# Moving a unit's part through the states next to the next unit's state sums

## Chip, cores, metric

One core of a Trainium2 chip. The metric is the device time of one execution in microseconds (us). Every run in this document was in the fast state, and every kernel timed or profiled gave correct results.

## The reference

```python
def _attn_ref(q, k, v, f_logit):                 # batch 4, heads 8, sequence 768, head_dim 48
    f = 1.0 / (1.0 + np.exp(-f_logit))
    for t in range(S):
        state = f[:, :, t, :, None] * state + np.einsum('bhd,bhe->bhde', k[:, :, t], v[:, :, t])
        y[:, :, t] = np.einsum('bhd,bhde->bhe', q[:, :, t], state)
def _moe_ref(x, w_a, w_b, w_out):                # 3072 x 384, d_ff 1536
    return ((x @ w_a) * (x @ w_b)) @ w_out       # x is y with its heads side by side
```

A gated linear attention feeds a bilinear feed-forward block. Everything is fp32.

## The kernel before

The attention is cut into 16 units of four heads and 384 positions. Head_dim is 48, so the attention's products use a quarter of the TensorE array, as 64-row tiles. The feed-forward's products use all of it (128x128 weights, 192 columns). They are the bulk of the work and are interleaved with the attention as "filler". The first units are written out by hand; from unit 4 on, a unit's work comes from this generator, whose pieces the scheduler takes up when its step counter passes the numbers given:

```python
    def slot(u):
        nxt = front(u + 1) if u + 1 < NU else iter(())
        next(nxt, None)
        yield
        if u > 2 * NQ:
            within(u - 1)        # L401: scores times v, 64-row, into ps_y
        if u < NU:
            scores(u)            # L319: k times q, 64-row, into ps_x; DVE masks
        next(nxt, None)
        yield
        if u < NU:
            turn(u)              # L347: six full 128x128 transposes; ACT copies kT (L351)
        if u > 2 * NQ:
            across(u - 1)        # L422: states times q, 64-row, adds into ps_y
        yield
        if u < NU:
            gains(u)             # L367: state sums, kT times v, 64-row; DVE adds
        yield
        # ... two more pieces of front(u + 1)

    def across(u):
        # ... L422 products into ps_y
        # ACT copies y out of ps_y in three copies (L435)
        # SyncE stores y into xT, the feed-forward's input (L450)
        # ... then load_unit(u + NSET): the loads of a later unit (L154, L156)
```

The filler is `up_pair` (L542, with ACT copies L550 to L559 and DVE adds L547) and `down` (L610). `down` writes its results into one tile `o` and stores that in two halves from SyncE (L645, L649). `begun_early` holds the step numbers of the first slots:

```python
        begun_early = (
            (22.9, 22.9, 24.5, 25, 26.3, 26.3),
            (27.3, 27.3, 27.8, 28.3, 29.8, 29.8),
            (30.3, 30.3, 31.3, 31.3, 32.3, 33.3),
            (33.4, 33.4, 33.9, 33.9, 36.1, 38.1),
            (39.1, 40.1, 41.1, 41.1, 42.1, 44.1),
        )
```

## Time and profile before

| | before |
|---|---|
| median of 3 runs | 630.34 us (629.26 to 631.24) |
| span of the profiled run | 628.2 us |
| PE busy | 592.5 us (94%) |
| DVE / ACT busy | 60% / 35% |

The prediction below shows and reads the lines that matter. Some things help in following it. PE is TensorE, ACT is ScalarE, DVE is VectorE, and SPq is the queue of SyncE, which issues transfers (DMA) here; tiles named ps_ are those that PE writes. A product of the program appears as two PE records (24 products of L422 as 48), a transpose as one. And the length of a PE record is modelled, so durations are read as differences of starts.

### The profile page before, as it was taken

What the parts mean: (1) busy time and instruction counts of PE and PEld (TensorE: products, weight loads), DVE (VectorE), ACT (ScalarE), POOL (GpSimd) and SP (SyncE); (2) the same over time, 40 slices, a digit from 0 to 9 for tenths busy, and PEclk for the clock granted to TensorE, in tenths of its full rate; (3) what the DMA queues carried; (4) which work ended last, traced back from release to release, by engine and by line L of the source; (5) the groups of instructions that cost most, each with busy time, mean ns of one, the idle gap of its engine ahead of it and who ended that gap; (6) DMA issues with size and microseconds to landing.
All of it is one profiled execution on the core that took longest, in us unless ns stands there. A gap on an engine that the chain in (4) does not pass through costs nothing.

```text
span 628.2 us, 13968 instructions
## 1 busy us (share of the span) xinstructions
PE 592.5 (94%) x5922; PEld 535.6 (85%) x5922; DVE 378.2 (60%) x748; ACT 221.3 (35%) x400; POOL 63.0 (10%) x58
## 2 busy tenths in 40 slices
PE   0859899999999999999999999999999999999995
PEld 0626555558998999999999999999999999999995
DVE  6868444797887567646675567647564344534541
ACT  6576498822332243224312242323311232022200
POOL 6243154410000000000000000000000000000000
PEclk9959999999999999999999999999999999999999
DMA  8786785000144404130404012040001000000000
GB/s 237 230 255 175 168 263 197 1 1 1 41 109 114 100 3 94 33 91 1 96 1 120 27 36 62 12 110 2 20 1 46 26 20 2 2 27 0 1 26 30
DMA packets 30343, 43.65 MB, mean 69 GB/s; under 512 B 3776, under 2 KB 24896, under 8 KB 30272
## 3 DMA queue, kind: packets, MB, share of 16 engines
q1 hardware_dynamic: 29984, 42.38, 25.0%
q8 instruction: 48, 0.79, 0.5%
q10 hardware_dynamic: 288, 0.30, 0.2%
q14 instruction: 23, 0.19, 0.1%
HBM read 33.23 MB, written 4.72 MB: 60 GB/s over the span
## 4 chain that ended last, share of the span: by engine, by line
PE 88%; DMA 4%; DVE 2%; ACT 2%; SPq 2%; issue 1%; ACTq 0%; DVEq 0%
PE ps_f L542 41%; PE ps_f L610 23%; PE ps_f L469 14%; DMA xT<-y 2%; PE ps_y L401 2%; PE ps_y L422 2%; PE ps_x L319 2%; PE ps_x L367 2%; PE ps_x L347 1%; SPq L154 1%; DMA raw<-in_moe_w_b_dram 1%; SPq L450 1%; DMA out_dram<-o 1%; ACT y L435 1%; DVE h L605 0%
## 5 line engine op out<-in xcount | busy, mean ns | idle before, releaser
L542 PE MATMUL ps_f<-xT,w_ba 128*128 128x192 f32 x864 | 155.4, 327 | 0.0
L547 DVE TENSOR_TENSOR groups<-ps_f,groups 128x384 f32<-128x384 f32 x144 | 80.1, 557 | 118.5 <-ACT groups L559 99.3
L542 PEld LDWEIGHTS ps_f<-xT,w_ba 128*128 128x128 f32 x864 | 142.3, 190 | 0.5
L469 PE MATMUL ps_f<-xT,w_ba 128*128 128x384 f32 x288 | 98.4, 502 | 7.9 <-DVE w_ba L216 5.9
L469 PEld LDWEIGHTS ps_f<-xT,w_ba 128*128 128x128 f32 x288 | 55.3, 195 | 47.8 <-DVE w_ba L216 7.0
L542 PE MATMUL ps_f<-b_sb,raw 128*128 128x192 f32 x432 | 82.0, 326 | 0.0
L542 PEld LDWEIGHTS ps_f<-b_sb,raw 128*128 128x128 f32 x432 | 72.2, 190 | 0.0
L550 ACT COPY groups<-ps_f 128x384 f32<-128x384 f32 x36 | 17.2, 478 | 109.3 <-PE ps_f L542 103.5
L610 PE MATMUL ps_f<-w_out,h 128*128 128x192 f32 x288 | 52.0, 330 | 0.3 <-DVE o L605 0.3
L610 PE MATMUL ps_f<-w_out,groups 128*128 128x192 f32 x288 | 50.9, 327 | 0.0
L610 PE MATMUL ps_f<-spare,h 128*128 128x192 f32 x288 | 49.6, 328 | 0.2 <-DVE h L605 0.2
L610 PEld LDWEIGHTS ps_f<-w_out,h 128*128 128x128 f32 x288 | 46.8, 190 | 1.3 <-DVE o L605 0.6
L610 PEld LDWEIGHTS ps_f<-w_out,groups 128*128 128x128 f32 x288 | 47.3, 190 | 0.1
L610 PEld LDWEIGHTS ps_f<-spare,h 128*128 128x128 f32 x288 | 46.7, 190 | 0.8 <-issue 0.5
L205 POOL TENSOR_SCALAR h<-h 128x768 f32<-128x768 f32 (+1 forms) x20 | 40.7, 2037 | 50.8 <-ACT h L202 50.8
L266 POOL TENSOR_SCALAR inv<-inv 128x768 f32<-128x768 f32 x14 | 13.5, 962 | 305.7 <-ACT inv L262 305.7
L605 DVE TENSOR_TENSOR o<-ps_f,u 128x192 f32<-128x192 f32 x36 | 12.8, 356 | 43.7 <-PE ps_f L610 40.8
L572 DVE TENSOR_TENSOR groups<-groups 128x384 f32<-128x384 f32 x72 | 36.6, 550 | 0.0
L559 ACT COPY groups<-ps_f 128x384 f32<-128x384 f32 x36 | 17.2, 478 | 52.7 <-PE ps_f L542 52.7
L542 PE MATMUL ps_f<-xT,raw 128*128 128x192 f32 x144 | 29.8, 330 | 0.0
L542 PE MATMUL ps_f<-b_sb,w_ba 128*128 128x192 f32 x144 | 29.3, 326 | 0.0
L319 PE MATMUL ps_x<-q_in,k_in 48*64 48x64 f32 x672 | 13.7, 226 | 16.2 <-DMA raw<-in_moe_w_b_dram 15.4
(113 smaller groups left out, 697.4 us busy)
## 6 DMA issues: line engine op xcount, KB each, us to landing
q_in<-in_q_dram SPq DMA_DIRECT2D x32, 144.0 KB, 4.0
k_in<-in_k_dram SPq DMA_DIRECT2D x32, 144.0 KB, 3.5
v_in<-in_v_dram SPq DMA_DIRECT2D x16, 288.0 KB, 5.1
raw<-in_moe_w_out_dram SPq DMA_DIRECT2D x6, 768.0 KB, 4.3
out_dram<-o SPq DMA_DIRECT2D x24, 192.0 KB, 1.9
f_in<-in_f_logit_dram SPq DMA_DIRECT2D x28, 144.0 KB, 3.0
xT<-y SPq DMA_DIRECT2D x46, 72.0 KB, 2.2
raw<-in_moe_w_b_dram SPq DMA_DIRECT2D x4, 768.0 KB, 7.2
```

What stands on the lines that cost most here:

```text
L205: nc.gpsimd.tensor_scalar(h, h, HI_MAX, None, ALU.min)
L266: nc.gpsimd.tensor_scalar(inv, inv, EXP_K, 1.0, ALU.mult, ALU.add)
L319: nc.tensor.matmul(ps[h][SUB * p:SUB * p + SUB, o:o + SUB], lhsT=kf[r, tokens(n, c, p)], rhs=qf[r, tokens(n, c, p)], start=True, stop=True,)
L367: nc.tensor.matmul(ps_x[R * h:R * h + D, p, (n * NC + c) * D:(n * NC + c) * D + D], lhsT=kT[r, n, c, R * h:R * h + D], rhs=t["v"][r, n, c, ...
L469: nc.tensor.matmul(ps[nm][:, 0:BLK], lhsT=w[:, kt, ft * 128:ft * 128 + 128], rhs=x[:, kt], start=kt == 0, stop=kt == NKT - 1,)
L542: nc.tensor.matmul(to[:, g], lhsT=w[:, g, j], rhs=x, start=start and g == 0, stop=True, skip_group_check=True)
L547: nc.vector.tensor_tensor(c[:, :, k, i], x, y, ALU.add)
L550: nc.scalar.copy(p1, x0)
L559: nc.scalar.copy(u3, x0)
L572: nc.vector.tensor_tensor(to[:, :, 2 * j + k], a[:, :, k], b[:, :, k], ALU.mult)
L605: nc.vector.tensor_tensor(to, x, y, op)
L610: nc.tensor.matmul(to, lhsT=x[:, i], rhs=w[:, i], start=first and i == 0, stop=i == HFT - 1, skip_group_check=True)
```

## The change

The states' part (`across`) moves from behind the transposes to just ahead of the next unit's state sums (`gains`). Both are 64-row products, so PE should enter and leave 64-row products twice a unit instead of three times.

```diff
         if u < NU:
             turn(u)
+        yield
         if u > 2 * NQ:
             across(u - 1)
-        yield
         if u < NU:
             gains(u)
```

## The prediction

> **What bounds the kernel now.** I read the page's busy shares first, then the table by stretches of time, then the list of instructions in order of time around the moved part, and last the SyncE queue. The first question is whether PE time is wall time where the change acts. In the table by stretches (columns: busy us and count of PE, PE's weight loads, DVE, ACT, POOL; granted clock; DMA share; GB/s):
>
> ```profile
> 60.00:147.00 87.00, 84.89 (x458) 50.47 (x460) 52.09 (x80) 57.87 (x84) 29.31 (x15) 1.00 0.41 116
> 147.00:205.00 58.00, 57.11 (x918) 54.39 (x908) 45.83 (x100) 16.13 (x32) 2.50 (x3) 1.00 0.29 73
> 205.00:540.00 335.00, 334.65 (x3453) 327.15 (x3452) 199.04 (x409) 94.83 (x195) 5.82 (x7) 1.00 0.17 42
> ```
>
> From 205 to 540 us PE is busy 334.65 of 335 us at full granted clock, DVE for 59% and ACT for 28%. PE is the bound there, and close to it from 147 to 205. The moved part runs only in those two stretches: the units before it, in the start-up, are written out by hand and are untouched. But "busy" says nothing of how densely PE issues, so I worked with starts. One unit of the attention (a unit is four heads of half a sequence), in PE's list in order of time (start, length, line, what, count; the length includes a modelled tail, so I use differences of starts):
>
> ```profile
> 325.98 0.89 PE L401 MATMUL ps_y<-at,v_in 64*48 64x64 f32 x48
> 326.69 0.92 PE L319 MATMUL ps_x<-q_in,k_in 48*64 48x64 f32 x48
> 327.54 2.22 PE L610 MATMUL ps_f<-w_out,h 128*128 128x192 f32 x12
> 329.59 0.82 PE L347 MATMUL ps_x<-ident,k_in 128*128 128x128 f32 x6
> 330.34 0.89 PE L422 MATMUL ps_y<-q_in,st 48*48 48x64 f32 x48
> 331.16 2.22 PE L610 MATMUL ps_f<-spare,groups 128*128 128x192 f32 x12
> 333.21 2.11 PE L610 MATMUL ps_f<-w_out,groups 128*128 128x192 f32 x12
> 335.26 0.74 PE L367 MATMUL ps_x<-v_in,kT 64*48 64x48 f32 x40
> ```
>
> L401 is the part within a block, L319 the scores, L347 the six transposes, L422 the part through the states (what moves), L367 the next unit's state sums. L610 and L542 are the big products of the other half of the kernel, interleaved as filler. The trace shows each fp32 product of the program as two records; I count records. A filler record costs 162.5 ns when undisturbed: in the same list elsewhere eight L542 records run from 203.87 to 205.17. So 12 should take 1.95 us, and what a stretch takes beyond that is the price of changing between full products and 64-row ones. Three changes into 64 rows are visible: at L401, L422, L367.
>
> **What the Trainium skill says.** "TensorEngine Tiling (Array Packing)", Key Properties: "Changing tiling mode (not just tile) drains the TensorE"; staying in a mode costs nothing of the kind. It gives no figure. The trace agrees and has the figures, about 0.1 us each, below. "TensorE: Matmul & The Clock Gate", Part 3, says products on different tiles of the array overlap and start some 4 ns apart; here 48 records of L422 start within 0.67 us, 14 ns apart on average, which agrees in kind. "Perfetto Trace Analysis", section Tensor Engine Instruction, says PE's end times are estimates, hence my use of starts, and that ACT and DVE are strictly in order, which matters for the rivals.
>
> **The change part by part.** No instruction is added or removed: 5,922 PE records stay. The comparison of the two programs' orders on PE shows nine places where L422 moves, always later, past 12 to 24 filler records. In eight of them it was directly after the transposes and now stands directly before L367. The ninth is the last unit, with no transposes before it and no sums after it. Three further units (those of about 185, 200 and 232 us) already had transposes, L422 and L367 in a row, so they don't change. The intent "two instead of three" thus holds for eight units, not twelve.
>
> What one of the eight saves, from starts:
> - Transposes followed by L422 took 330.34 - 329.59 = 0.75 us. Where a unit had no L422 (149.59, below) transposes followed by filler took 150.24 - 149.59 = 0.65. Saved: 0.093 (with the starts at ns).
> - L422 followed by filler took 331.16 - 330.34 = 0.82. A 64-row group followed by another 64-row group is L401 before L319: 326.69 - 325.98 = 0.71, and the same L401 followed by filler, in the last unit (506.59 to 507.40 below), takes 0.82. Saved: 0.110. L401 and L422 use the same order of tiles, so I take this over to L422 before L367.
> - Filler after L422 has one slow step besides: 24 records from 331.16 to 335.26 take 4.10 = 3.90 + 0.20, while in 149 to 153 us, with transposes before, 12 records take 2.04 = 1.95 + 0.094. The 0.094 is the entry into L367, which stays (as the entry into L422). Saved: 0.104.
>
> ```profile
> 149.59 0.82 PE L347 MATMUL ps_x<-ident,k_in 128*128 128x128 f32 x6
> 150.24 2.12 PE L610 MATMUL ps_f<-w_out,h 128*128 128x192 f32 x12
> 152.28 0.76 PE L367 MATMUL ps_x<-v_in,kT 64*48 64x48 f32 x48
> ...
> 506.59 0.89 PE L401 MATMUL ps_y<-at,v_in 64*48 64x64 f32 x48
> 507.40 1.57 PE L542 MATMUL ps_f<-xT,w_ba 128*128 128x192 f32 x8
> ```
>
> Sum 0.307 us a unit; all of it on PE, the bound. Eight units: **2.46 us**.
>
> There is one side gain. SyncE's queue is in order, and in the unit of 330 us it now holds an output store back behind the moved part's stores and the next loads:
>
> ```profile
> 332.31 3.79 SPq L450 DMA_DIRECT2D xT<-y  x5
> ...
> 339.16 0.42 SPq L156 DMA_DIRECT2D v_in<-in_v_dram  x1
> 339.68 0.42 SPq L649 DMA_DIRECT2D out_dram<-o  x1
> ...
> 343.86 0.36 DVE L605 TENSOR_TENSOR o<-ps_f,u 128x192 f32<-128x192 f32 x1 [2.84 <-DMA out_dram<-o]
> 344.27 1.89 PE L610 MATMUL ps_f<-w_out,h 128*128 128x192 f32 x10 [0.28 <-DVE o L605]
> ```
>
> DVE waits to write the single output tile o until that store has landed, and PE waits for DVE: 12 filler records from 341.88 to 344.27 take 2.39 instead of 1.95. In the changed program's SyncE order this L649 stands before the L450 stores. Its data is ready at 333.84 (end of the DVE step), so it should land near 336, eight us before it is needed. Gain **0.44 us**, once.
>
> One small loss: ACT copies y out after L422 in three copies (1.46 us), and the first-half copy of the next pair of products (L550, 0.48 us) now comes behind them in the last unit, with only filler between. Copies end about 2.4 us after L422 starts (475.76 + 1.46 against 474.80 in the unit of 474), L550 at 2.9; PE needs it 12 records after filler resumes: 0.82 + 0.10 + 1.95 = 2.87. With a semaphore's delay, up to 0.1 us. In the units that move before a pair, L367 lies between (0.67 us), so slack is 0.5.
>
> Sum: 2.46 + 0.44 - 0.1 = 2.8 us of 630.34.
>
> **The rivals.**
> 1. L367 waits where it now stands. Against the 36 ns assumed between L422 and L367, the three units that have them in a row show some 0.29 us (L422's last start to L367's first). But there the transposes' copy kT ends just before: in the unit of 185 us ACT's L351 runs 185.29 to 186.08 and L367 starts at 186.14. In the changed order 12 to 24 filler records, 2 to 4 us, lie between the copy and its reader. If the 0.29 was the array's after all, the saving is 0.05 a unit, and the time is 629.5.
> 2. ACT or the transfers become the bound: y's copies now collide with copies that the next products need, and xT arrives 2 to 4 us later. Against: the slack above; xT of the unit at 297 us lands near 305 and is read at 348; the last unit's lands at 518.8 and is read at 546. The next loads of the unit at 167 us move 2 us: f would land near 178 and is read at 179.5, the tightest of all. If several slipped, half a us each, the time is 629 to 631.
> 3. PE isn't the bound and nothing moves. The first fence speaks against it.
> 4. All three removed terms are larger than the neighbours tell, or more waits resolve like the one at 344 us (PE has one more of 0.8 us at 195, where the scores wait for DVE; that chain starts from PE, so it shifts along): 626.
>
> **Range and chances.** 630.34 - 2.8 = **627.5 us**, 0.4% less. The three timed runs of before spread over 2 us, which is most of the uncertainty; the medians of two kernels may differ by 1 us from that alone. Rivals 1 and 2 pull up to 629.5. Range 626.0 to 629.3. Faster by over 2% would need 12.6 us, more than all changes of mode together: 0.01. Slower by over 2% would need a new wait of 15 us: 0.01.
>
> **What would show it right or wrong.** In PE's list of the changed kernel: transposes to filler 0.65 us; L422 to L367 0.71 instead of 0.82 to filler; filler after transposes without the extra 0.2; at about 341 us no wait of DVE on out_dram. Wrong if L422 to L367 takes 0.95 as in rival 1, if a filler stretch after L367 shows a step over 0.3 us released by ACT, or if scores or L526 wait on DMA.

## The result

The kernel after took 626.58 us (median of 4 runs, 625.93 to 627.19) against 630.59 for the kernel before, measured beside it (629.26 to 631.24, 4 runs). The ratio is 0.9939, with a 95% interval from 0.9919 to 0.9959: a gain of 0.6%, small but clear of the noise. Ratios here are the mean time of one kernel's fast runs over that of the other's in the same rounds, so not quite the ratio of the medians. Both kernels were run again, twice for after: ratios 0.9943 (0.993 to 0.9956) and 0.9939 (0.9926 to 0.9952). The predicted 627.5 lay 0.9 us above the measured median; the predicted gain of 2.8 us stands against 3.6 to 3.8 by these ratios.

The same unit as in the prediction's second fence, in PE's list in order of time of the kernel after (start, length, what, count):

```profile
325.40 2.22 PE L610 MATMUL ps_f<-w_out,h 128*128 128x192 f32 x12
327.46 0.82 PE L347 MATMUL ps_x<-ident,k_in 128*128 128x128 f32 x6
328.11 2.12 PE L610 MATMUL ps_f<-spare,groups 128*128 128x192 f32 x12
330.07 2.11 PE L610 MATMUL ps_f<-w_out,groups 128*128 128x192 f32 x12
332.11 0.89 PE L422 MATMUL ps_y<-q_in,st 48*48 48x64 f32 x48
332.82 0.71 PE L367 MATMUL ps_x<-v_in,kT 64*48 64x48 f32 x40
```

The transposes now hand over to filler after 327.46 to 328.11 = 0.65 us (0.75 to L422 before). The 24 filler records take 332.11 - 328.11 = 4.00 (4.10). L422 hands over to L367 after 0.71 (0.82 to filler). L367 itself took 335.26 to 335.93 = 0.67 before and takes 332.82 to 333.46 = 0.64 now. The first three are the prediction's three terms; the fourth it didn't have. In five of the eight units the starts of L422 and L367 mix (last section), so the 0.71 can be read in three only; from transposes to the filler after L367 all eight gain 0.33 to 0.34 us.

SyncE in the same stretch of the kernel after, to be read against the prediction's fourth fence:

```profile
330.72 0.35 SPq L649 DMA_DIRECT2D out_dram<-o  x1
334.08 3.05 SPq L450 DMA_DIRECT2D xT<-y  x5
337.17 1.06 SPq L154 DMA_DIRECT2D f_in<-in_f_logit_dram  x2
```

The output store L649 goes out at once, ahead of the stores of y and the loads. PE's wait near 344 us is gone. After 205 us PE has only one step of over 0.3 us left in the kernel after, 0.54 us at 537, and that one is in both kernels.

The price was where the prediction put it, in the last unit. ACT's list of the kernel after there:

```profile
511.41 1.46 ACT L435 COPY y<-ps_y 128x384 f32<-128x384 f32 x3 [2.91 <-PE ps_y L422]
512.90 0.48 ACT L550 COPY groups<-ps_f 128x384 f32<-128x384 f32 x1
513.58 0.48 ACT L553 COPY groups<-ps_f 128x384 f32<-128x384 f32 x1 [0.20 <-ACT groups L550]
```

L550 has no idle time before it: it stood ready behind the three copies of y. It ends at 513.38 and PE's next product into that bank starts at 513.43. The stretch of 8 records from 512.68 to 514.19 takes 1.51 us instead of 1.30, so 0.2 us are lost.

### The profile page after: what moved, and what is told of

Its sections match the earlier page's. It is cut to its first block, busy times and chain, and to the rows that moved or that the text cites. A ratio compares the mean times of both kernels' runs of the same rounds, so it can differ in the third digit from the quotient of the medians.

```text
span 624.1 us, 13969 instructions
## 1 busy us (share of the span) xinstructions
PE 588.6 (94%) x5922; PEld 534.5 (86%) x5922; DVE 377.8 (61%) x748; ACT 221.6 (36%) x400; POOL 63.0 (10%) x58
## 4 chain that ended last, share of the span: by engine, by line
PE 89%; DMA 4%; ACT 2%; DVE 2%; SPq 1%; issue 0%; ACTq 0%; DVEq 0%
PE ps_f L542 42%; PE ps_f L610 25%; PE ps_f L469 14%; DMA xT<-y 2%; PE ps_x L319 2%; PE ps_y L401 2%; PE ps_x L367 2%; PE ps_y L422 1%; PE ps_x L347 1%; DMA raw<-in_moe_w_b_dram 1%; DMA q_in<-in_q_dram 1%; SPq L154 1%; DVE h L605 0%; SPq L150 0%; ACTq L450 0%
## 5 line engine op out<-in xcount | busy, mean ns | idle before, releaser
L610 PE MATMUL ps_f<-w_out,h 128*128 128x192 f32 x288 | 51.8, 330 | 0.0
L550 ACT COPY groups<-ps_f 128x384 f32<-128x384 f32 x36 | 17.2, 479 | 94.9 <-PE ps_f L542 94.8
L610 PE MATMUL ps_f<-w_out,groups 128*128 128x192 f32 x288 | 50.9, 327 | 0.0
L610 PE MATMUL ps_f<-spare,h 128*128 128x192 f32 x288 | 49.4, 327 | 0.2 <-DVE h L605 0.2
L610 PEld LDWEIGHTS ps_f<-w_out,groups 128*128 128x128 f32 x288 | 47.4, 190 | 0.1
L610 PEld LDWEIGHTS ps_f<-w_out,h 128*128 128x128 f32 x288 | 46.8, 190 | 0.6
L610 PEld LDWEIGHTS ps_f<-spare,h 128*128 128x128 f32 x288 | 46.8, 190 | 0.7 <-issue 0.5
L435 ACT COPY y<-ps_y 48x384 f32<-48x384 f32 (+1 forms) x43 | 20.5, 476 | 25.9 <-PE ps_y L422 21.5
```

The lines of the kernel that those rows point to most:

```text
L435: copy(y[r:r + rows, :, p], ps[p][e:e + rows, 0:BLK].rearrange("r (o m) -> r o m", m=SUB))
L550: nc.scalar.copy(p1, x0)
L610: nc.tensor.matmul(to, lhsT=x[:, i], rhs=w[:, i], start=first and i == 0, stop=i == HFT - 1, skip_group_check=True)
```

## The experiments

All kernels share the start-up, which ends where the scores at about 146 us start. I call the rest, from there to the end of the span, the **scheduled part**. It is read from each run's profile. It includes a tail, from the start of PE's last product to the end of the span, that took 6.36 to 6.62 us in the twelve profiles; differences of up to 0.26 us can come from there, and where it matters times are given up to the last product. Each diff is against the kernel before in stores_late and against the kernel after in the others.

### Before and after again

No edit. The two first profiles left something open: their scheduled parts differ by 481.53 - 478.58 = 2.95 us, the medians by 4.0.

> The unchanged kernel before, for its spread. In the two profiles at hand the scheduled part (from the first record of the scores at about 146 us to the end of the span) took 481.53 us before and 478.58 after, 2.95 less, but the measured medians differ by 4.0 us; the other 1.1 us lie in the start-up, before any moved instruction (those scores start at 146.67 before, 145.53 after). Theory A, the start-up differs by chance from run to run: this run's scheduled part is 481.5 within 0.1, and its start-up anything from 145 to 148. Theory B, the change makes the start-up shorter by 1.1 us in some way: the start-up is within 0.3 of 146.7 here and of 145.5 in after_again.

> The unchanged kernel after. Theory A: scheduled part 478.6 within 0.1, start-up anything from 145 to 148, time over five rounds 2.5 to 3.5 us under before. Theory B: start-up within 0.3 of 145.5, time 4.0 under before.

| run | start-up ends at | scheduled part | median (runs) |
|---|---|---|---|
| before, first profile | 146.67 | 481.53 | |
| before_again | 146.39 | 482.28 | 629.96 (13) |
| after, first profile | 145.53 | 478.58 | |
| after_again | 147.23 | 478.50 | 626.56 (5) |

Theory A holds for the start-up: it was later in after_again than in before_again, so these profiles show no shortening by the change. For the scheduled part A was wrong about the kernel before, which was not 481.5 but 0.75 more. Its trace shows why. This is the list in order of time around the output store in before_again:

```profile
340.03 0.42 SPq L649 DMA_DIRECT2D out_dram<-o  x1
...
341.65 2.11 PE L610 MATMUL ps_f<-w_out,groups 128*128 128x192 f32 x12
...
344.53 0.36 DVE L605 TENSOR_TENSOR o<-ps_f,u 128x192 f32<-128x192 f32 x1 [3.74 <-DMA out_dram<-o]
...
344.94 0.76 PE L610 MATMUL ps_f<-w_out,h 128*128 128x192 f32 x3 [1.18 <-DVE o L605]
```

The 12 filler records from 341.65 to 344.94 take 3.29 us instead of 1.95: a wait of 1.34 against 0.44 in the first profile. Counted from the first half's store (L645), L649 went out 0.59 us later than in the first profile and took 0.32 us longer to land (4.38 against 4.06): together the 0.9 that the wait is longer. The tail after the last product was 0.27 shorter, which hides part of it. So how late the store behind the loads lands varies from run to run. None of the three profiles of the kernel after has the wait, so the change gains more than the one profile showed.

### stores_late: the transfers' half of the change alone

PE's, ACT's and DVE's order stay as before (so the traces show, record by record). Only the stores of y and the loads behind them move to the later place:

```diff
-        y = y.rearrange("r (n c) p m -> r n (c p m)", n=2)
+        live[u]["out"] = y.rearrange("r (n c) p m -> r n (c p m)", n=2)
+        if u <= 2 * NQ - 1:
+            ship(u)
+    def ship(u):              # the stores L450 and load_unit(u + NSET)
...
         yield
+        if u > 2 * NQ:
+            ship(u - 1)
         if u < NU:
             gains(u)
```

> The kernel before, where only the stores of y to xT and the loads that follow them are moved to the later place (SyncE's order is then that of after; PE's, ACT's and DVE's are those of before). Theory: the wait of PE for the output store at 344 us goes (it cost 0.604 - 0.163 = 0.44, and 0.10 for the slow restart after it), and nothing else: scheduled part 481.53 - 0.55 = 480.98. Rival, the gain of the unit at 330 us comes from PE's own order: 481.5, with the wait still there.

Scheduled part 480.77 us; median 629.28 (22 runs) against 630.19 for before (51 runs), ratio 0.9987 (0.998 to 0.9994). PE in the stretch of the wait, in this run's list (lines are 5 higher here, L615 is L610):

```profile
341.67 2.11 PE L615 MATMUL ps_f<-w_out,groups 128*128 128x192 f32 x12
343.62 2.11 PE L615 MATMUL ps_f<-w_out,h 128*128 128x192 f32 x12
```

The 12 records take 1.95 us, with no wait, although PE's order is that of before. The scheduled part lies 0.2 under the 480.98 expected only through its tail: up to PE's last product it took 474.36 us against 474.91 before, just the 0.55 expected. So this part of the gain is the transfers' order and nothing of PE's. The ratio puts its mean over many runs at 0.0013 x 630 = 0.8 us (0.4 to 1.3), between the two profiles' waits.

### split_within: as many changes of mode as before, at another place

```diff
         next(nxt, None)
-        yield
         if u > 2 * NQ:
             within(u - 1)
+        yield
         if u < NU:
             scores(u)
```

> The kernel after, where the part within a block (L401) is moved one place earlier, away from the scores (L319), so that eight units change into 64-row products three times again, at another place. Theory, each stay in 64-row products costs 0.31 us whatever is in it: 478.58 + 8 x 0.31 = 481.1, L401 takes 0.82 to filler instead of 0.71 to the scores. Rival, the gain of the change was a matter of the states' part and its neighbours (kT copy, y copies): 478.6 to 479.

Scheduled part 480.95 us, against 481.1 expected by the theory; median 629.59 (21 runs), ratio 0.9991 (0.9983 to 0.9999), where after_again on the same chip had 0.9943. PE's list:

```profile
287.33 0.89 PE L401 MATMUL ps_y<-at,v_in 64*48 64x64 f32 x48
288.14 0.92 PE L542 MATMUL ps_f<-xT,raw 128*128 128x192 f32 x4
288.90 2.11 PE L542 MATMUL ps_f<-xT,w_ba 128*128 128x192 f32 x12
290.94 0.93 PE L319 MATMUL ps_x<-q_in,k_in 48*64 48x64 f32 x48
```

L401 takes 0.81 us to filler, not 0.71, and the 16 filler records take 290.94 - 288.14 = 2.80 instead of 2.60. The cost follows the number of stays in 64-row products, not the states' part or its copies.

### three_in_a_row: two changes a unit, got the other way

```diff
         if u < NU:
             turn(u)
-        yield
         if u > 2 * NQ:
             across(u - 1)
         if u < NU:
             gains(u)
         yield
+        yield
```

> Two changes into 64-row products a unit as in after, but got the other way: the states' part stays after the transposes and the state sums (L367) are moved up to it, so that all three stand in a row in every unit, as they already did in three. Theory: L367 then waits for ACT's copy of kT (0.8 us), 0.29 us from L422's last start to L367's first instead of 0.04, in eight more units: 8 x 0.25 = 2.0 back of what the change gained, the output store of the unit at 330 us is late again (0.55 to 1.45), and the last unit's 0.2 loss goes: scheduled part (from the scores at about 146 us to the end) 478.5 + 2.0 + 1.0 - 0.2 = 481.3. Rival, only the count of mode changes matters: 478.5 to 479.5.

Scheduled part 483.67 us; median 631.65 (21 runs) against 629.74 (28), ratio 1.0034 (1.0022 to 1.0047): slower than before, and 2.4 us more than the theory gave. The waits that it named are there: in eleven units L367 starts 0.29 to 0.30 us after L422's last start, released by kT. What I had left out are three others. This is the list in order of time of one of those units, and of the unit that has no states' part:

```profile
260.76 1.46 ACT L435 COPY y<-ps_y 128x384 f32<-128x384 f32 x3
260.77 0.76 PE L367 MATMUL ps_x<-v_in,kT 64*48 64x48 f32 x48
261.45 2.22 PE L610 MATMUL ps_f<-spare,h 128*128 128x192 f32 x12
...
263.39 0.40 DVE L390 TENSOR_SCALAR st<-st,f_in 128x48 f32<-128x48 f32 x2
263.71 0.35 DVE L605 TENSOR_TENSOR u<-ps_f,u 128x192 f32<-128x192 f32 x1
264.09 0.36 DVE L605 TENSOR_TENSOR u<-u,u 128x192 f32<-128x192 f32 x1
264.11 1.57 PE L610 MATMUL ps_f<-w_out,groups 128*128 128x192 f32 x8 [0.44 <-DVE u L605]
```

```profile
149.16 0.82 PE L347 MATMUL ps_x<-ident,k_in 128*128 128x128 f32 x6
150.87 0.76 PE L367 MATMUL ps_x<-v_in,kT 64*48 64x48 f32 x48 [0.89 <-ACT kT L351]
```

In the first, DVE's adds of the state sums now come ahead of the two adds that PE's next filler needs, and PE waits (0.7 us with its restart, also in the unit at 409 us). In the second, L367 stands directly behind the transposes, with nothing to cover the kT copy at all (about 1.0 us dearer than in the kernel after). From transposes to the filler after L367, without the filler between, a unit took 2.38 us instead of 2.10 in the kernel after, nearly all of it the wait for kT. With 8 x 0.28 for that, 1.0 for the store (its wait is in this trace at 345 us), and the last unit's 0.2 won back, that sums to 2.2 + 1.0 + 1.4 + 1.0 - 0.2 = 5.4. Measured were 483.67 - 478.5 = 5.2, with a tail that was 0.2 to 0.3 shorter than in the kernel after. So the count of mode changes is not enough: the filler between the transposes and L367, which the change under study leaves in place, covers waits that are dearer than the changes of mode saved.

### all_units and all_units_b: the rest of what the change aimed at

all_units is the kernel after with filler between transposes and states' part in the three units that didn't have it, and the last unit's states' part put back where ACT has time for its copies. all_units_b also delays one unit's scores past a wait for DVE.

```diff
             turn(u)
+        elif u > 2 * NQ:
+            across(u - 1)
         yield
-        if u > 2 * NQ:
+        if 2 * NQ < u < NU:
             across(u - 1)
...
-            (30.3, 30.3, 31.3, 31.3, 32.3, 33.3),
-            (33.4, 33.4, 33.9, 33.9, 36.1, 38.1),
-            (39.1, 40.1, 41.1, 41.1, 42.1, 44.1),
+            (30.3, 30.3, 30.8, 31.3, 32.3, 33.3),
+            (33.4, 33.4, 33.9, 34.4, 36.1, 38.1),    # all_units_b: (33.4, 33.9, 34.4, 35.4, 36.1, 38.1)
+            (39.1, 40.1, 41.1, 42.1, 42.1, 44.1),
```

> The kernel after, with filler put between the transposes and the states' part in the three units that have all three in a row (185, 200, 232 us), and the last unit's states' part back at its old place. Theory: three waits for kT of 0.25 us go, and the last unit's wait for ACT of 0.2: scheduled part 478.5 - 0.95 = 477.6, time 626.56 - 0.95 = 625.6. Rival, the 0.29 us in those three units is not the wait for kT: no change there, 478.3.

> As all_units, with the unit at about 193 us begun one filler stretch later, so that its scores no longer wait 0.91 us for DVE's keys. Theory: that wait goes, scheduled part 477.6 - 0.9 = 476.7 and 624.7 us. Rival, DVE's chain starts from PE there and what follows moves with it, or another wait takes its place: 477.6 or more.

all_units: scheduled part 477.28, median 625.12 (8 runs), ratio 0.9938 (0.9916 to 0.996). All three kT waits are gone, and so is the last unit's. It gained 1.2 us on after's 478.5, where 0.95 was expected; 0.15 of that is a shorter tail.

all_units_b: scheduled part 476.59, median 625.39 (6 runs), ratio 0.9932 (0.9906 to 0.9958). The wait for DVE is gone. Part of it came back: filler waits at 198 us for an ACT copy (L642) that now stands behind the next unit's two activations. The list in order of time:

```profile
197.19 0.84 ACT L264 ACTIVATE f_in<-f_in 128x768 f32<-128x768 f32 x1
...
197.94 0.30 ACT L642 COPY o<-ps_f 128x192 f32<-128x192 f32 x1
...
198.29 1.89 PE L610 MATMUL ps_f<-spare,groups 128*128 128x192 f32 x10 [0.23 <-ACT o L642]
```

By the trace this version is 0.7 us better; its median was not. So both ran once more beside the kernel after, on one chip.

> The kernel after once more, on one chip and in the same rounds as the two that may beat it: 626.6, scheduled part 478.5 within 0.1.

> all_units in the same rounds: scheduled part 477.3 (as in its first run), so 1.2 us under after_third. Rival, its first run was lucky by its start-up: within 0.4 of after_third.

> all_units_b in the same rounds: scheduled part 476.6, so 0.7 under all_units_2 and 1.9 under after_third. Its first run measured 625.39 against 625.12 of all_units, which theory A lays to the start-up (146.98 against 146.12 in the two profiles); the rival is that the new wait for ACT at 198 us is as dear in most runs as the wait for DVE that it took away.

| run | start-up ends at | scheduled part | median (6 runs each) | ratio to before (95%) |
|---|---|---|---|---|
| after_third | 147.70 | 478.46 | 627.12 | 0.9939 (0.9926 to 0.9952) |
| all_units_2 | 146.51 | 477.34 | 625.97 | 0.9927 (0.9915 to 0.9939) |
| all_units_b_2 | 146.81 | 476.58 | 625.91 | 0.9921 (0.9906 to 0.9936) |

The scheduled parts repeat within 0.1 us and put all_units_b 1.9 us ahead of after and 0.7 ahead of all_units. The times agree in order, but their intervals overlap; the step between the last two is not resolved by them. Both versions beat the kernel before, and all_units_b is the best by the trace.

### What could not be tried

A second tile `o` in the kernel before would have taken the store's wait away in another way. It doesn't fit: the build stopped with 21.3 KB a partition left for the pool `raw`, where 24 were needed. stores_late took its place.

## Why the prediction was right

- **PE is the bound, so PE's time is wall time.** Right. The scheduled part of after came out at 478.46, 478.50 and 478.58 us in three profiles, and the terms below account for the difference. In the two first profiles they do so almost to the last digit: eight units gained 2.70 us in all, the store's wait 0.55; the last unit lost 0.21 and four units' scores (L319) took 0.01 to 0.03 longer, 0.10 in all. That makes 2.94, and up to PE's last product the two kernels differ by 474.91 - 471.97 = 2.94.
- **Three terms, 0.307 us a unit.** Right, each at the predicted size (0.65, 0.71, 0.094 instead of 0.2 beside the filler). In all a unit saves slightly more: from transposes to the filler after L367 the unit at 297 us took 301.73 - 296.71 = 5.02 before and takes 299.60 - 294.92 = 4.68 after, 0.34. The 0.03 is L367's own. split_within confirmed the size from the other side: 480.95 - 478.5 = 2.45 for eight more stays, 0.31 each. And stores_late and after, which have the same order of transfers, differ by 474.36 - 471.97 = 2.39 up to the last product, the 2.70 less the two losses.
- **Eight units, not twelve.** Right. The three units already in a row saved nothing; all_units shows what was left in them.
- **The output store, 0.44 us.** Right in mechanism (stores_late shows it alone), too small in size. In that very profile the slow restart after the wait adds 0.10. In before_again the wait was 1.34, and the mean by stores_late is 0.8. It was one draw of a varying wait, and I took it for a constant.
- **The last unit's ACT copies, up to 0.1.** Right in mechanism, 0.2 in size: the wait itself and again the slow restart.
- **Rival 1** (L367 would wait at its new place) fell for this order: 0.04 us from L422's last start in three units, and in the other five L367 starts before L422 is through. three_in_a_row shows that the wait for kT is real as soon as the filler is taken out.
- **Rival 2** (ACT or transfers become the bound) showed only in the last unit. **Rival 4** (waits resolve as well) is what the store's wait partly did.

Sum with the measured terms: 2.7 + 0.8 - 0.2 = 3.3 us. The three ratios say 3.6 to 3.8, with intervals of 0.8 to 1.3 us either way. What remains lies within each of those; the start-up varied by 2.2 us over all profiles (145.53 to 147.70). So the predicted gain of 2.8 was about a quarter short of the ratios. Some 0.5 of that is the sizes above, the store's wait above all; the rest is not explained beyond the spread of the runs.

## What to carry to other kernels

When small products are strewn among full ones on a PE-bound stretch, count the stays in the small mode, price one from starts in the trace (here 0.31 us), and join neighbours; but leave filler between a transpose and the product that reads its copy, or the wait eats the gain. Compare the order of every in-order queue, not only of the engine that the change is about: about a quarter of this gain (0.8 of 3.3 us) came from a store that slipped ahead of loads. And a wait on a transfer, seen once in a profile, is one draw; look at a second run before putting a number on it.

## What the Trainium skill lacked or had wrong

- "TensorEngine Tiling (Array Packing)", Key Properties, says that a change of tiling mode drains TensorE but gives no cost. Here one stay in 64-row products between full ones cost 0.31 us: 0.094 to enter, 0.110 to leave, 0.104 at the second full record after leaving.
- "TensorE: Matmul & The Clock Gate", Part 3, has products strictly in order at start and end. In the kernel after, five of the eight joined units start some L367 records ahead of L422 records that come before them in the program (PE's list in order of time; ends are modelled, so only the starts are shown):

```profile
298.27 0.71 PE L422 MATMUL ps_y<-q_in,st 48*48 48x64 f32 x34
298.80 0.21 PE L367 MATMUL ps_x<-v_in,kT 64*48 64x48 f32 x1
298.81 0.22 PE L422 MATMUL ps_y<-q_in,st 48*48 48x64 f32 x2
```

- The same page, Part 3, gives starts some 4 ns apart on different tiles; the median here was 7 ns, and 14 on average over a group of 48 records of L422.
- No page that I read prices the restart after a wait: in six waits between full products (344 us in both profiles of before, 513 in after, 264, 345 and 409 in three_in_a_row) the second record after the wait starts 0.266 to 0.267 us after the first instead of 0.163, so each cost 0.10 more than its idle time. It is not always so much: after the wait at 541 us in before the step is 0.237.
